# First batch fetched by whole slots, the first weight quarter between its loads, the others behind a gate

One core of one Trainium2 chip. The metric is the device time of one execution in microseconds (us); shorter is better.

## The reference

```python
X = np.fft.fft(x, axis=1)           # x: 8 batches of 3008 rows of 256
X = np.fft.fft(X, axis=2).real
h = np.maximum(X.reshape(24064, 256) @ w_in, 0.0)   # w_in: 256 x 2048
out = h * h @ w_out                                 # w_out: 2048 x 256
```

The kernel folds each batch by symmetry (a row is added to its mirror row), does the first transform as matmuls with cosine and sine tables ("first stage", tiles `pf`), puts the second transform into the weights (`G`, made from `w_in` by the `pc`/`ps` matmuls), multiplies by `G` (`xb`), squares, and multiplies by `w_out` (`po`).

## The kernel before

`x4` holds a batch in four slots: 0 and 1 are the upper rows of each half (fetched by SP), 2 and 3 the mirror rows (gathered by GpSimd). A fold adds slot `s` to slot `3 - s`, so slots 0 and 3 are the first pair and 1 and 2 the second.

```python
    for q in (0, QH):                          # two halves of three rows per partition
        for s in range(2):
            gather_half(0, 1 - s, QH - q)      # 378 KB, 3 KB rows
            nc.sync.dma_start(out=x4[0:NP, s, q : q + QH, :], in_=up(0, s, q, QH))
        if q == 0:
            load_mid(0, nc.sync)
            ...
    # fold_ops(0): for each half h, both pairs, then what hangs on that half
    return [[pair(0, h), pair(1, h), pair0(h * QH, QH), half(h, 0), edges(0, h * QH, QH)]
            + [feat(i, h * QH, QH) for i in (0, 2)] for h in range(2)], odd
    ...
    for f in mi0[0:0] + [dmats_fin, lambda: load_w_in(0, 1, 2, 3)] + mi0[0:] + [dmats_hi] + fe[0]:
        f()
    for f in rd1[0:0] + fe[1][0:3] + [lambda: load_x(1)] + fe[1][3:]:
        f()
    load_w_out()                               # GpSimd's queue, behind batch 1's gathers
    ...
    gcast(0, nc.scalar.copy)
    ...
    s1[0](); warm_up(2); gmat(0); s1[1](); s1[2]()    # first half, weight quarter 0, second half
```

The `po` matmuls of an output tile are ordered so:

```python
            cut = NFC if grp is final else NFC - 2 * nf
            ops += [one(grp, j, fc) for fcs in (range(cut), range(cut, NFC))
                    for j in range(len(grp)) for fc in fcs]
```

## Time and profile before

| | before |
|---|---|
| time, first chip | 606.13 us median of 4 (605.12 to 606.29) |
| profiled execution | 604.28 us, faster than all four of these; span 602.2 us, of which TensorE 581.0 busy |
| last gather of batch 0 landed | 16.48 us |
| first stage starts / first `xb` matmul | 13.40 / 21.51 us |
| `w_out` pieces landed | 36.89, 38.28, 39.64, 41.02 us |
| third group of four `po` matmuls | 39.98 us |

Landings are the completion records in the trace: each gather and each piece of `w_out` has 16 of them (here and there one is missing), and the last one counts.

### The profile page before, as it was taken

How to read it: one execution, taken by the hardware profiler on the slowest of the kernel's cores; microseconds unless marked ns; L12 is line 12 of the kernel's file. 1: busy time of each engine (PE TensorE's matmuls, PEld its weight loads, DVE VectorE, ACT ScalarE, POOL GpSimd, SP SyncE). 2: the span in 40 equal slices, each digit the busy share in tenths (PEclk: the TensorE clock that was granted, in tenths of full speed). 3: DMA queues.
4: the chain of work that ended last, by engine and by line, in shares of the span. 5: the costliest groups of instructions: out<-in, count | busy, mean ns of one | idle time of the engine just before them, and what ended most of it. 6: DMA issues, size and time to landing. Idle time of an engine off the chain costs nothing.

```text
span 602.2 us, 12242 instructions
## 1 busy us (share of the span) xinstructions
PE 581.0 (96%) x4543; PEld 436.9 (73%) x4543; DVE 522.6 (87%) x959; ACT 548.6 (91%) x963; POOL 164.4 (27%) x156
## 2 busy tenths in 40 slices
PE   2879999999999999999999999999999999999997
PEld 1556677777777777777777778777787778877786
DVE  6888898998898998898898997899889899999880
ACT  7789899999989999989998989999998999999981
POOL 5301022023322122312023043412443423324400
PEclk9989999999999999999999999999999999999999
DMA  8985484564483414913233115133242231332112
GB/s 237 283 105 155 109 238 149 175 234 54 63 246 54 62 46 73 244 41 45 56 60 45 53 38 63 42 45 58 58 63 41 50 53 54 44 62 56 56 53 71
DMA packets 42232, 56.24 MB, mean 93 GB/s; under 512 B 7774, under 2 KB 36754, under 8 KB 42174
## 3 DMA queue, kind: packets, MB, share of 16 engines
q1 hardware_dynamic: 37310, 42.04, 33.0%
q0 software_dynamic: 4864, 13.44, 8.7%
q8 instruction: 35, 0.57, 0.4%
q14 instruction: 23, 0.19, 0.1%
HBM read 29.02 MB, written 24.64 MB: 89 GB/s over the span
## 4 chain that ended last, share of the span: by engine, by line
PE 91%; DMA 4%; ACT 1%; POOL 1%; issue 1%; DVE 1%; POOLq 0%; ACTq 0%; DVEq 0%
PE po L74 54%; PE xb L74 31%; PE pf L74 6%; DMA wout<-in_moe_w_out_dram 3%; DMA x<-in_x_dram,idx 2%; POOL x L99 0%; POOL x L112 0%; ACT h L747 0%; ACT os L618 0%; ACT h L726 0%; ACT bs L713 0%; DVE bs L716 0%; DVE h L727 0%; DVE h L697 0%; ACT h L748 0%
## 5 line engine op out<-in xcount | busy, mean ns | idle before, releaser
L74 PE MATMUL po<-wout,h 128*128 128x256 f16 x3024 | 451.1, 273 | 3.5 <-DMA wout<-in_moe_w_out_dram 3.0
L74 PEld LDWEIGHTS <-h 128*128 128x128 f16 x3024 | 286.5, 98 | 113.8 <-issue 5.0
L74 PE MATMUL xb<-qt,G 128*128 128x512 f16 (+10 forms) x743 | 207.7, 322 | 1.3 <-ACT h L671 1.0
L714 POOL TENSOR_TENSOR bs<-bs,h 128x512 f32<-128x512 f32 x92 | 118.6, 1292 | 316.0 <-ACT bs L713 254.8
L727 DVE CUSTOM_DVE_ANT_0 h<-xb,bs 128x512 f16<-128x512 f32 (+1 forms) x231 | 144.6, 638 | 22.9 <-ACT h L726 22.1
L74 PE MATMUL xb<-pt,G 128*128 128x512 f16 (+16 forms) x512 | 146.7, 324 | 1.0 <-DVE h L727 0.4
L726 ACT ACTIVATE h<-xb 128x512 f16<-128x512 f32 (+1 forms) x218 | 135.4, 623 | 7.8 <-PE xb L74 5.5
L74 PEld LDWEIGHTS <-G 128*128 128x128 f16 x1255 | 120.5, 98 | 24.2 <-issue 2.8
L750 DVE TENSOR_TENSOR h<-h 128x2048 f16<-128x2048 f16 (+1 forms) x113 | 137.0, 1214 | 0.8 <-ACT h L738 0.7
L671 ACT ACTIVATE h<-xb 128x512 f16<-128x512 f32 (+1 forms) x166 | 103.8, 629 | 9.3 <-PE xb L74 8.4
L738 ACT ACTIVATE h<-xb 128x512 f16<-128x512 f32 (+2 forms) x155 | 95.8, 622 | 10.1 <-PE xb L74 8.5
L716 DVE SCALAR_TENSOR_TENSOR bs<-xb,h 128x512 f32<-128x512 f32 (+1 forms) x126 | 82.9, 659 | 18.7 <-PE xb L74 15.4
L748 ACT ACTIVATE h<-h 128x1024 f16<-128x1024 f16 (+1 forms) x79 | 84.8, 1074 | 0.0
L747 ACT ACTIVATE h<-h 128x1024 f16<-128x1024 f16 (+1 forms) x79 | 83.6, 1059 | 0.1
L697 DVE TENSOR_SCALAR h<-eb,gE 128x512 f16<-128x512 f16 (+1 forms) x198 | 69.9, 368 | 0.0
L618 ACT ACTIVATE os<-po 128x512 f32<-128x512 f32 (+1 forms) x95 | 59.5, 626 | 8.9 <-PE po L74 8.9
L713 ACT ACTIVATE bs<-xb 128x512 f32<-128x512 f32 x92 | 57.3, 623 | 3.2 <-PE xb L74 2.0
L112 POOL DMA_INDIRECT x<-in_x_dram,idx x16 | 21.0, 1314 | 78.8 <-DVE u L364 62.0
L360 DVE TENSOR_TENSOR u<-x 127x765 f16<-127x765 f32 x32 | 30.2, 965 | 3.5 <-DMA x<-in_x_dram,idx 3.5
L74 PEld LDWEIGHTS <-w 127*128 127x128 f16 (+1 forms) x192 | 22.1, 119 | 7.7 <-DVE w L373 2.2
L373 DVE TENSOR_TENSOR w<-v 127x384 f16<-127x384 f16 x64 | 22.1, 369 | 0.0
L74 PE MATMUL pf<-cosT,w 127*128 127x377 f16 (+1 forms) x96 | 20.6, 329 | 1.3 <-DVE w L373 1.3
(111 smaller groups left out, 212.5 us busy)
## 6 DMA issues: line engine op xcount, KB each, us to landing
out_dram<-os SPq DMA_DIRECT2D x157, 128.0 KB
x<-in_x_dram SPq DMA_DIRECT2D x14, 756.0 KB
wst<-in_moe_w_in_dram SPq DMA_DIRECT2D x4, 512.0 KB
eb<-qt SPq DMA_DIRECT2D x14, 128.0 KB
x<-in_x_dram SPq DMA_DIRECT2D x4, 378.0 KB
wout<-in_moe_w_out_dram POOLq DMA_DIRECT2D x4, 256.0 KB, 17.3
x<-in_x_dram,idx POOLq DMA_INDIRECT x20, 9.6
gE<-G SPq DMA_DIRECT2D x16, 0.2 KB
```

The source lines that it names most:

```text
L74: nc.tensor.matmul(o, l, r, start=start, stop=stop, skip_group_check=True)
L618: act(os_[:, js], po[:, js], AF.Copy, bias=0.0, scale=HS * HS)
L671: act(r_s(c, u), xb, AF.Relu, scale=-1.0)
L697: ts(out=X, in0=ebc[c][:, 0:n], scalar1=gE2[:, u : u + 1], scalar2=None, op0=ALU.mult)
L714: nc.gpsimd.tensor_tensor(T, T, X, op=ALU.add)
L716: stt(out=T, in0=xb, scalar=-2.0, in1=X, op0=ALU.mult, op1=ALU.add)
L726: act(r_s(c, u), xb, AF.Relu, scale=-1.0)
L727: mirrors.append((int(DEFER[c][u]), lambda: relu_d(c, u, lambda o, i: nc.vector._custom_dve(TENSOR_ADD_SAT, out=o[:, 0, :], in0=xb[:, 0, i ...
L738: relu_d(c, u, lambda o, i: act(o, xb[:, :, i], AF.Relu, scale=-1.0))
L747: act(h2[:, 0:nf], h2[:, 0:nf], AF.Square)
L748: rest.append(lambda: act(h2[:, nf:], h2[:, nf:], AF.Square))
L750: vt(h2, h2, h2, op=ALU.mult)
```

## The change

Its intent: longer rows for the first batch's loads, the weight that TensorE needs first brought in earlier, and the other weights kept from competing with the batch.

```diff
-    for q in (0, QH):
-        for s in range(2):
-            gather_half(0, 1 - s, QH - q)
-            nc.sync.dma_start(out=x4[0:NP, s, q : q + QH, :], in_=up(0, s, q, QH))
-        if q == 0:
+    for s in range(2):
+        gather(0, 1 - s)
+        nc.sync.dma_start(out=x4[0:NP, s, :, :], in_=up(0, s))
+        if s == 0:
             load_mid(0, nc.sync)
+            load_w_in(0)
 ...
-            return [[pair(0, h), pair(1, h), pair0(h * QH, QH), half(h, 0), edges(0, h * QH, QH)]
+            return [([pair(0, 0), pair(0, 1)] if h == 0 else [])
+                    + [pair(1, h), pair0(h * QH, QH), half(h, 0), edges(0, h * QH, QH)]
 ...
+    def w_gate():
+        for c in range(1, 4):
+            nc.vector.memset(wst[c][:, 0, 0:1], 0.0)   # the loads must wait for these writes
+        load_w_in(1, 2, 3)
 ...
-    for f in mi0[0:0] + [dmats_fin, lambda: load_w_in(0, 1, 2, 3)] + mi0[0:] + [dmats_hi] + fe[0]:
+    for f in mi0[0:0] + [dmats_fin] + mi0[0:] + [dmats_hi] + fe[0][:2] + [w_gate] + fe[0][2:]:
         f()
-    for f in rd1[0:0] + fe[1][0:3] + [lambda: load_x(1)] + fe[1][3:]:
+    for f in rd1[0:0] + fe[1][0:2] + [lambda: load_x(1)] + fe[1][2:]:
```

(Cut: the scratch tile moved from weight buffer 0 to 1, one index vector gone, a rewritten list that has the same values.)

More of the change, by code (lines that the diff above doesn't have):

```diff
@@ L80, in iota @@
         return t
-    idx3 = iota("idx3", [P, 1], [[0, 1]], NQ // QH * (NP - 1), -(NQ // QH), I32)
+    idx = iota("idx", [P, 1], [[0, 1]], NP - 1, -1, I32)
     pidx = iota("pidx", [P, 1], [[0, 1]], 0, 1)
@@ L96, in up @@
                        ap=[[NQ * D, NP], [1, n * D]])
-    def gather_half(b, s, q):
-        nc.gpsimd.indirect_dma_start(
-            out=x4[0:NP, 2 + s, q : q + QH, :].rearrange("p q d -> p (q d)"),
-            out_offset=None,
-            in_=bass.AP(tensor=x.tensor, offset=x.offset,
-                        ap=[[QH * D, B * S // QH], [1, QH * D]]),
-            in_offset=bass.IndirectOffsetOnAxis(ap=idx3[0:NP, 0:1], axis=0),
-            element_offset=(b * S + (s + 1) * M - NQ * NP + q) * D)
     def gather(b, s):
@@ L140, with load_w_in @@
     wst = [h2p.tile([P, 2, F // 4], F32, name="wst", tag="h2") for _ in range(4)]
-    jm = wst[0].rearrange("p c f -> p (c f)")[:, 0 : 3 * P].rearrange("p (a b) -> p a b", a=3)
-    for q in (0, QH):
-        for s in range(2):
-            gather_half(0, 1 - s, QH - q)
-            nc.sync.dma_start(out=x4[0:NP, s, q : q + QH, :], in_=up(0, s, q, QH))
-        if q == 0:
+    jm = wst[1].rearrange("p c f -> p (c f)")[:, 0 : 3 * P].rearrange("p (a b) -> p a b", a=3)
+    def load_w_in(*quarters):
+        for c in quarters:
+            cs = slice(c * F // 4, (c + 1) * F // 4)
+            nc.sync.dma_start(out=wst[c],
+                              in_=moe_w_in[:, cs].rearrange("(c p) f -> p c f", p=P))
+    for s in range(2):
+        gather(0, 1 - s)
+        nc.sync.dma_start(out=x4[0:NP, s, :, :], in_=up(0, s))
+        if s == 0:
             load_mid(0, nc.sync)
+            load_w_in(0)
             jrow = jm[:, 0]
@@ L150 @@
                            allow_small_or_imprecise_dtypes=True)
-    idx = iota("idx", [P, 1], [[0, 1]], NP - 1, -1, I32)
     idx2 = iota("idx2", [P, 1], [[0, 1]], NQ // 2 * (NP - 1), -NQ // 2, I32)
@@ L755 @@
     rd1, tr1, mi1 = table_ops(1)
-    def load_w_in(*quarters):
-        for c in quarters:
-            cs = slice(c * F // 4, (c + 1) * F // 4)
-            nc.sync.dma_start(out=wst[c],
-                                in_=moe_w_in[:, cs].rearrange("(c p) f -> p c f", p=P))
+    def w_gate():
+        for c in range(1, 4):
+            nc.vector.memset(wst[c][:, 0, 0:1], 0.0)
+        load_w_in(1, 2, 3)
     def load_w_out():
@@ L825 @@
     for c in range(1, F // 512):
-        side.setdefault(c * (c - 1) // 2, []).extend([lambda c=c: gmat(c), lambda c=c: gneg(c)])
+        side.setdefault((0, 1, 3)[c - 1], []).extend([lambda c=c: gmat(c), lambda c=c: gneg(c)])
     spread(rd1[0:], 0, 5)
```

## The prediction

> **What bounds the kernel now.** I read the page's busy shares first, then its chain of work that ended last, then that chain in order of time for the first 45 us, then the timelines of VectorE and TensorE there, and a table of windows over the same stretch.
>
> ```profile
> PE 581.0 (96%) x4543; PEld 436.9 (73%) x4543; DVE 522.6 (87%) x959; ACT 548.6 (91%) x963; POOL 164.4 (27%) x156
> ...
> PEclk9989999999999999999999999999999999999999
> DMA  8985484564483414913233115133242231332112
> ...
> PE 91%; DMA 4%; ACT 1%; POOL 1%; issue 1%; DVE 1%; POOLq 0%; ACTq 0%; DVEq 0%
> ```
>
> TensorE is busy for 581.0 of 602.2 us, so only 21 us are idle in all. The change touches only the load and fold of the first batch and the load of the first weight, so only the first 42 us can change, and at best they give back a part of those 21 us. A gain of 2% (12 us) is out of reach from here. The chain of work tells what rules this head:
>
> ```profile
> 5.29 9.62 DMA x<-in_x_dram,idx
> ...
> 17.85 1.22 POOL x L112
> 19.37 1.03 POOL x L112
> 20.40 0.83 POOL wout L766
> 21.23 17.05 DMA wout<-in_moe_w_out_dram
> 38.28 0.04 issue
> 38.33 1.01 PE po L74 x4
> ```
>
> From 5 us to 38 us it is transfers: the first batch, then its slots are free and batch 1 is fetched, then w_out queues up behind batch 1's gathers. TensorE waits for w_out here:
>
> ```profile
> 34.27 0.27 PE L74 MATMUL xb<-qt,G 128*128 128x256 f16 x1
> 36.93 0.60 PE L74 MATMUL po<-wout,h 128*128 128x256 f16 x4 [2.39 <-DMA wout<-in_moe_w_out_dram]
> ...
> 38.33 1.01 PE L74 MATMUL po<-wout,h 128*128 128x256 f16 x4 [0.58 <-DMA wout<-in_moe_w_out_dram]
> ...
> 41.27 0.77 PE L74 MATMUL po<-wout,h 128*128 128x256 f16 x4
> ```
>
> The four pieces of w_out landed at 36.89, 38.28, 39.64 and 41.02 us (landing records of the trace), and the groups of four po matmuls start at 36.93, 38.33, 39.98 and 41.27. So the fourth piece pins TensorE to about 41.3 us, whatever happened before. The windows say that the transfer engines were full all the way, and that the wait let the clock drop:
>
> ```profile
> core 0: us, PE busy (x) PEld busy (x) DVE busy (x) ACT busy (x) POOL busy (x), PEclk, DMA share, GB/s
> ...
> 21.50:34.50 13.00, 11.58 (x84) 8.18 (x84) 12.86 (x24) 12.70 (x24) 2.13 (x3) 1.00 1.20 228
> 34.50:38.30 3.80, 0.86 (x7) 0.58 (x6) 3.77 (x11) 3.80 (x9) 0.00 (x0) 0.99 1.29 157
> 38.30:41.60 3.30, 3.27 (x16) 2.28 (x16) 2.50 (x9) 2.61 (x8) 0.00 (x0) 0.50 0.46 39
> ```
>
> [...] while both queues have work (6 to 14 us) they share some 260 GB/s, and a 3 KB packet of the SP queue takes 121 ns alone (median, 2 to 4 us) and 167 ns beside gathers (9 to 13 us). [...] Here the granted clock goes to full at 17.7 us, and is 0.50 in 38.2 to 41.6, after the w_out wait. [...] the 127x765 fold takes 955 ns whatever the row length of its load, so the change makes no fold cheaper. [...] the 128x128 int32 operation took 1.70 us at 7.93, ending as the zeroing of ez (7.90, 1.39 us) was over.
>
> **The change, part by part.** On VectorE only the order changes, as the two kernels' instruction orders show; the only additions are three 128x1 memsets (60 ns each, as the one at 1.40 us), 0.2 us in the shade of a DMA wait. TensorE and ScalarE keep their order; the rearranged list of weight groups (0, 1, 3) equals c(c-1)/2.
>
> Loads. Before, SP issues four 378 KB pieces, GpSimd four gathers; now two of 756 KB each. GpSimd saves two gathers of 1.0 to 1.1 us. The bytes are the same (3.1 MB). Packets of gathers were already 6 KB for the most part; SP's grow from 3 KB to 6 KB. In batch 2's load at 52 us, SP's 6 KB rows alone ran at 234 ns a packet (26 GB/s per engine) against 25 GB/s for 3 KB rows, and 289 GB/s over whole microseconds, against 353. So I count no gain from longer rows. What counts is the order of bytes. First pair: up to 5.4 us SP's slot (before, the two half slots landed at 4.34 and 5.46), with the gather complete at some 8.2 to 9 us (774 KB from 4.3 us, at some 200 GB/s beside the smaller weight packets). Second pair: it must follow 3.1 MB and 0.52 MB of the first weight quarter. Before, the transfers had moved 3.62 MB at 14.2 us and the last gather landed at 16.48. I put the second pair at 14.7 us (estimate, 14.2 to 15.5): about 1.8 us earlier, as three weight quarters (issued at 10.16 before) no longer share.
>
> Folds. Before, the last piece cost one pair fold: 16.50 + 0.95 + 0.18 + 0.56 + 0.17 + 0.62, with overlaps, 18.88.
>
> ```profile
> 14.94 0.95 DVE L360 TENSOR_TENSOR u<-x 127x765 f16<-127x765 f32 x1 [1.33 <-DMA x<-in_x_dram,idx]
> 16.50 0.95 DVE L360 TENSOR_TENSOR u<-x 127x765 f16<-127x765 f32 x1 [0.60 <-DMA x<-in_x_dram,idx]
> 17.37 0.18 DVE L364 TENSOR_TENSOR u<-x 127x6 f16<-127x6 f32 x1
> 17.58 0.56 DVE L369 TENSOR_TENSOR v<-u 127x768 f16<-127x768 f16 x1
> ```
>
> Now both halves' folds follow the last landing: 2 x (0.95 + 0.18 + 0.56 + 0.17 + 0.62) = 5.0 us, less small overlaps. First half ready (its first feature) at 14.7 + 2.2 = 16.9, second at 19.6. So TensorE's first stage starts at 16.9 instead of 13.40, cold: nine matmuls of 0.31 us, two warm-ups of 0.43, four weight matmuls of 0.43, nine more: 8.2 us at half clock, some 6.4 us [...]. It ends at 23.3 us instead of 21.3: a loss of 2.0 us there. The first weight quarter, for which ScalarE sat idle 3.8 us, lands early; that wait goes.
>
> Slots. Batch 1's load is issued when the last pair fold and its edge are done: 14.7 + 0.1 + 3.6 = 18.4 against 17.58. But before, three quarters of a megabyte of weights were still queued in front of it; now some 0.1 MB is. Bytes up to then: 5.19 MB (batch and weights) moved at 19.7 us before, and now at 18.5, with up to 1 us of hole until batch 1's first packet (an SP load took 1.0 us from issue to packet, a gather 2.3). From there w_out ends a chain of the same bytes. If bytes decide, w_out's last piece comes about 0.5 us sooner; if the gathers' late start decides, 0.8 us later. I take 0.5 sooner, 40.5 us.
>
> Sum. TensorE reaches its first w_out wait at 34.5 + 2.0 = 36.5, so the 2 us lost in the first stage are taken out of a wait of 3.0 us and cost nothing; the idle stretch gets shorter, and the clock probably stays full. TensorE after the fourth piece: 41.27 before (with 0.16 us more lost until the clock rose at 41.6), 40.6 now: some 0.9 us gained. 606.16 - 0.9 = 605.2 us.
>
> **Rivals.** (a) TensorE becomes the bound: first piece used at 36.5 or later, then 2.2 us of work at full clock to the fourth group, 38.7. Only if w_out comes over 1.8 us sooner does this matter; it caps the gain at 2.7 us: 603.5. For it: 0.65 MB less backlog before batch 1, at 300 GB/s 2 us. Against it: the hole, and batch 1's gathers, that needed until 35.87 to land. (b) The late slots win: gathers of batch 1 start with the slots at 18.4 to 19.5 and w_out keeps its 23.5 us distance (17.55 to 41.02): 41.9, a loss of 0.5: 606.7. For it: gathers crept at 6 to 61 KB per us for the first four us even when their queue had work. (c) The second pair lands no earlier than 16.5, since 6 KB rows of both queues beside each other ran at 240 to 250 GB/s in 22 to 28 us with 390 ns a packet: then everything is 1.8 us later, TensorE reaches po at 38.3, and w_out too comes later: up to 607.5.
>
> **Range and chances.** The mechanisms move the fourth piece by +1 to -2 us; (b) and (c) bound one side, (a) the other[...]. Range 603.6 to 606.9. Faster by over 2% needs 12 us, more than the head's idle time holds: 1%. Slower by 2%: 1%. Within 2%: 98%.
>
> **What would show it.** Right: the pair folds at some 9 and 10 us and again at 15; first stage start near 17; no ScalarE wait for the weight; batch 1 issued near 18.4; the TensorE wait for w_out down from 3.0 to under 1.5 us with no half clock near 40; fourth w_out piece at 40 to 41. Wrong: the second pair after 16.5, w_out's fourth piece later than 41.5, or a new wait of TensorE between 23 and 36 us (a weight quarter not there, as they were gated).

## More of the kernel before

All that matters here happens in the first 45 us. From there on TensorE is nearly always busy: from the third group of `po` matmuls to the end, the fourteen traces of this study take 561.5 to 562.9 us.

## The result

The changed kernel took 606.8 us (median of 4, 606.3 to 607.13) against 606.13. The ratio of fast runs is 1.0014, with a 95% interval of 0.9997 to 1.0031: the same at 2%, and not a gain. On another chip, with 6 and 11 runs, it was 607.31 against 604.33, ratio 1.0055 (1.0039 to 1.0071): slower by 3.3 us. A ratio here is the mean time of one kernel's fast runs over that of the other's of the same rounds, so not quite the ratio of the medians. I take the second as the better measure, with more runs. On the chips of the three sets below the kernel before had medians of 604.04, 604.33 and 603.05, and its profiled execution took 604.28, so its four runs at 606.1 were probably on its slow side and flatter the change; as chips may differ, that is likely and not shown.

The page of the changed kernel: busy shares, slices, and the chain by engine.

```profile
PE 579.3 (96%) x4543; PEld 436.1 (72%) x4543; DVE 524.1 (87%) x962; ACT 547.7 (91%) x963; POOL 163.1 (27%) x153
...
DMA  8793685674484314913133115133342231332112
...
PE 87%; DMA 5%; ACT 4%; DVE 1%; POOL 1%; issue 1%; ACTq 0%; DVEq 0%; POOLq 0%
```

TensorE has less busy time (579.3 against 581.0, as less of it ran slowly: at a clock of 0.50 from 20.8 to 23.8 us, where before its matmuls were as slow from 13.4 to 17 us and the clock was 0.50 from 38.2 to 41.6) in a longer span (604.5 against 602.2). ScalarE's part of the chain grew from 1% to 4%. One of the waits of the first 46 us (engine, line, what it waited for, us in total, times, longest):

```profile
PE po L74 <- DMA wout<-in_moe_w_out_dram: 0.9, 3, 0.4
```

The wait for `w_out` fell from 3.0 to 0.9 us, as forecast. But TensorE sat idle 11.1 us for the first fold. VectorE's folds and TensorE's first stage in order of time (start, duration; in brackets the idle time before it, and what ended that):

```profile
10.06 1.81 DVE L356 TENSOR_TENSOR u<-x 127x765 f16<-127x765 f32 x2
11.82 0.08 DVE L756 MEMSET wst<- 128x1 f32 x3
18.60 0.96 DVE L356 TENSOR_TENSOR u<-x 127x765 f16<-127x765 f32 x1 [6.70 <-DMA x<-in_x_dram,idx]
...
20.97 0.95 DVE L356 TENSOR_TENSOR u<-x 127x765 f16<-127x765 f32 x1
```

```profile
20.84 1.13 PE L74 MATMUL pf<-cosT,w 127*128 127x377 f16 x3 [11.12 <-DVE w L369]
...
26.87 0.27 PE L74 MATMUL xb<-pt,G 128*128 128x256 f16 x1 [0.26 <-DVE pt L490]
...
42.80 0.60 PE L74 MATMUL po<-wout,h 128*128 128x256 f16 x4 [0.36 <-DMA wout<-in_moe_w_out_dram]
```

The same three points of TensorE in the kernel before:

```profile
13.40 1.12 PE L74 MATMUL pf<-cosT,w 127*128 127x377 f16 x3 [1.31 <-DVE w L373]
...
21.51 0.27 PE L74 MATMUL xb<-pt,G 128*128 128x256 f16 x1 [0.26 <-DVE pt L493]
...
39.98 1.06 PE L74 MATMUL po<-wout,h 128*128 128x256 f16 x4
```

The second pair landed at 18.58 us, 2.1 us later than the last gather before. The first stage starts 7.4 us later and the first `xb` 5.4 us later. The third `po` group is at 42.80 instead of 39.98, and that difference of 2.8 us, less some 0.8 that the kernel before lost there at half clock (an estimate: half of the 1.6 us from 39.98 until its clock rose at 41.6), is most of the 2.3 us between the two spans. The windows of the two kernels, before first and the changed one after it (window, length, busy time of TensorE, its weight loads, VectorE, ScalarE and GpSimd, clock, share of the transfer engines, GB/s). In the first line the clock of 1.00 is no reading up to 17.7 us, since the trace's clock records start there:

```profile
16.00:19.50 3.50, 1.99 (x8) 0.70 (x7) 2.93 (x7) 1.14 (x2) 1.34 (x2) 1.00 1.04 377
19.50:23.00 3.50, 2.98 (x18) 1.70 (x17) 2.14 (x6) 3.20 (x6) 3.50 (x5) 1.00 1.00 267
```

```profile
16.00:19.50 3.50, 0.00 (x0) 0.00 (x0) 0.90 (x2) 0.00 (x0) 0.00 (x0) 0.50 0.99 321
19.50:23.00 3.50, 2.16 (x7) 1.19 (x8) 3.29 (x12) 0.00 (x0) 0.68 (x1) 0.50 0.23 85
```

Before, the transfers were full all the way (share 1.04 and 1.00). Now there is a hole at 19.5 to 23 us (share 0.23): the weights are all but through (0.15 MB of packets after 20 us) and batch 1 is not asked for before 22.0 us, since the late folds still hold its slots. Everything behind the hole, `w_out` last, comes about 3 us later (third piece 42.76 instead of 39.64).

### The profile page after: what moved, and what is told of

It is laid out like the page before. It is cut to its first block, busy times and chain, and to the rows that moved or that the text cites. A ratio compares the mean times of both kernels' runs of the same rounds, so it can differ in the third digit from the quotient of the medians.

```text
span 604.5 us, 12238 instructions
## 1 busy us (share of the span) xinstructions
PE 579.3 (96%) x4543; PEld 436.1 (72%) x4543; DVE 524.1 (87%) x962; ACT 547.7 (91%) x963; POOL 163.1 (27%) x153
## 4 chain that ended last, share of the span: by engine, by line
PE 87%; DMA 5%; ACT 4%; DVE 1%; POOL 1%; issue 1%; ACTq 0%; DVEq 0%; POOLq 0%
PE po L74 52%; PE xb L74 30%; PE pf L74 6%; DMA wout<-in_moe_w_out_dram 3%; DMA x<-in_x_dram,idx 2%; ACT h L723 1%; ACT h L744 1%; POOL x L103 1%; ACT h L745 1%; ACT os L615 0%; ACT bs L710 0%; DVE h L724 0%; DVE u L356 0%; POOL wout L762 0%; DVE h L694 0%
## 5 line engine op out<-in xcount | busy, mean ns | idle before, releaser
L103 POOL DMA_INDIRECT x<-in_x_dram,idx x18 | 24.0, 1332 | 83.2 <-DVE u L360 66.0
L74 PE MATMUL pf<-cosT,w 127*128 127x377 f16 (+1 forms) x96 | 20.7, 329 | 11.1 <-DVE w L369 11.1
```

The costliest lines, as they stand in the source:

```text
L74: nc.tensor.matmul(o, l, r, start=start, stop=stop, skip_group_check=True)
```

## The experiments

Two explanations of the loss had to be told apart: `w_out` lands late because of the hole (transfers), or TensorE's first stage is late and nothing hides it any more (compute). And for the late second pair: weights let in too early, long rows, or the order of slots. Twelve kernels ran, all correct, five rounds each, in three sets of four, each set on one chip. Ratios are to the kernel before on that chip. The set's chip had it at a median of 604.04 (first), 604.33 (second) and 603.05 (third).

**1. The gate one fold later**, in the changed kernel: no quarter but the first can move before the second pair is in.

```diff
-    ... + fe[0][:2] + [w_gate] + fe[0][2:]:
+    ... + fe[0][:3] + [w_gate] + fe[0][3:]:
```

> The changed kernel with its gate moved one fold later, behind the first fold of the second pair, so that no other weight quarter can start before that pair is in. Theory A (weights let in too early): the changed kernel's last gather landed at 18.6 us because the gate opened at 11.8 us and 0.97 MB of weights moved ahead of it; without them 3.62 MB at 273 KB per us land at about 15 us, first stage of TensorE near 17.5 us (20.84 in the changed kernel), the hole in the transfers at 20 to 23 us gone, third piece of w_out near 40 us instead of 42.8, time 1 to 2 us under the changed kernel. Rival B (6 KB rows are slow): last gather stays at 17.5 us or later and the time within 0.5 us of the changed kernel.

Ratio 1.0078 (1.0055 to 1.0100), 609.24 us: the slowest of all. The second pair landed at 16.66 instead of 18.58, so early weights did cost 1.9 us. But that is far from 15 us, and the time went the other way. Its windows:

```profile
12.00:16.00 4.00, 0.00 (x0) 0.00 (x0) 0.00 (x0) 3.53 (x9) 0.00 (x0) 1.00 0.67 212
16.00:19.50 3.50, 0.55 (x2) 0.28 (x3) 2.68 (x10) 0.00 (x0) 0.00 (x0) 1.00 0.13 36
```

The hole did not vanish; it moved forward and grew, because the weights were asked for only after the landing (the gate opened at 17.59 us) and their traffic began at 18.8 us and filled the transfer engines only from 19.5 us. The first stage was 1.9 us earlier than in the changed kernel (18.95), the third `po` group later (43.9, behind a `w_out` wait of 2.3 us and at half speed: `xb` matmuls 0.21 us apart after it, 0.11 before). An earlier first stage is worth nothing while `w_out` comes late.

**2. The first weight quarter behind both slots**, in the changed kernel.

```diff
         if s == 0:
             load_mid(0, nc.sync)
-            load_w_in(0)
             ...
+    load_w_in(0)
```

> The changed kernel with the first weight quarter issued behind both slots instead of between them; gate as it is. Theory A counts bytes: half a megabyte less ahead of the second pair, so it lands at about 16.6 us instead of 18.6; time about 1 us under the changed kernel, the hole shorter by 1 to 2 us. Rival B (row length): no change of the landing beyond 0.5 us.

Ratio 1.0043 (1.0023 to 1.0062). The second pair landed at 16.19, 2.4 us sooner and so the expected size, the hole shrank to about 1.2 us, first `xb` 24.95, third `po` group 40.3. Its profiled execution (604.85 us) was its fastest; its other five were at 606.4 to 607.8. It is within 0.12% of the control in the next set, on another chip, so no gain in time over the changed kernel is shown.

**3. Half slots in 3 KB rows**, in the changed kernel: four loads and four gathers, in the same order of slots.

```diff
-        gather(0, 1 - s)
-        nc.sync.dma_start(out=x4[0:NP, s, :, :], in_=up(0, s))
+        for q in (0, QH):
+            gather_half(0, 1 - s, QH - q)
+            nc.sync.dma_start(out=x4[0:NP, s, q : q + QH, :], in_=up(0, s, q, QH))
```

> The changed kernel with each slot loaded as two halves in 3 KB rows, in the same order of slots, weight and gate as it is. Theory A: rows do not matter, last gather at 18 to 19.5 us, time within 0.7 us of the changed kernel. Rival B: last gather at 16.5 us or earlier, and about 1 us faster than the changed kernel.

Ratio 1.0013 (0.9994 to 1.0032), on the chip where edit 2 had 1.0043 and edit 1 had 1.0078. Both expectations missed. The last piece landed at 17.66, 0.9 us sooner. But the fold did not wait for it:

```profile
15.63 0.95 DVE L367 TENSOR_TENSOR u<-x 127x765 f16<-127x765 f32 x1 [2.69 <-DMA x<-in_x_dram,idx]
...
18.00 0.95 DVE L367 TENSOR_TENSOR u<-x 127x765 f16<-127x765 f32 x1
```

A fold needs one half of each slot. When each half is its own transfer it starts when that half is in, at 15.63; with whole slots it waits for all of both, 18.60. So the first stage starts at 17.87 instead of 20.84. Whole slots cost 3.0 us here: some 2 by their grain, and 0.9 by the later landing. Whether that 0.9 is the row length or the gate, which opened at 12.87 us here and at 11.82 in the changed kernel, was not separated. Long rows alone do not make the landing late: edit 2 has them and landed at 16.19.

**4. The gate alone**, in the kernel before: quarters 1 to 3 behind the last pair fold.

```diff
-    ... [dmats_fin, lambda: load_w_in(0, 1, 2, 3)] ...
+    ... [dmats_fin, lambda: load_w_in(0)] ...
-    ... fe[1][0:3] + [lambda: load_x(1)] ...
+    ... fe[1][0:2] + [w_gate] + fe[1][2:3] + [lambda: load_x(1)] ...
```

> The kernel before with only the gate added: weight quarters 1 to 3 wait for the last pair fold. Theory A: last gather at about 14.7 us instead of 16.5, second half of the fold done near 17 us; but the transfers were full before and stay full, so w_out comes no earlier (third piece at 39.6, within 0.7 us) and the time stays within 0.6 us of the kernel before. Rival C (the end is set by how late the folds and the first stage are): 1.5 to 2 us faster than the kernel before.

Ratio 1.0044 (1.0023 to 1.0064). The last gather landed at 16.55 instead of 16.48: keeping the weights out gained nothing at all. A gather counts as landed with its last share: its 16 completions came in from 13.30 to 16.55 us. A hole of some 3 us opened between 15.5 and 19 us, and TensorE waited 3.65 us for the fourth quarter, which now landed at 29.9. Both expectations missed: the landing did not move, and the time got worse by 2.9 us. (The same loads landed at 16.48, 16.65 and 15.73 us in three executions, so differences under 1 us in one trace are noise; the changed kernel had 18.58, 18.47 and 18.49.)

**5 and 6. `w_out` ahead of batch 1**, in the kernel before and in the changed kernel.

```diff
+    def w_out_first():
+        for c in range(4):
+            nc.vector.memset(wout16[:, c * NFC // 4, 0:1], 0.0)
+        load_w_out()
-    ... + [lambda: load_x(1)] + ...
+    ... + [w_out_first, lambda: load_x(1)] + ...
-    load_w_out()
```

A control, the changed kernel itself, ran beside them:

> The changed kernel once more, as a control on the same chip as the next runs. Ratio to the kernel before between 1.0005 and 1.003, as in the first result; third group of po matmuls at 42 to 43.5 us; a hole in the transfers at 20 to 23 us.

It had 1.0055, more than expected; its third `po` group was at 42.5 and the hole was there.

> The kernel before with w_out fetched ahead of batch 1's gathers (gated by one-column zeroings behind the last pair fold). Theory D (the end of the head is the third piece of w_out; what comes before it hides behind that wait): w_out lands before 33 us, TensorE waits for it no more, third group of po matmuls near 36 to 38 us instead of 40.0, 2 to 4 us faster than the kernel before (ScalarE and VectorE are full between 27 and 40 us, which eats a part of the 4.7 us). Rival C (the first stage sets the end already): no change beyond 0.7 us.

Ratio 0.9948 (0.9932 to 0.9964), 600.98 us, the best time. No `po` matmul waits for `w_out` any more, and the third group comes at 38.32.

> The changed kernel with the same edit. Theory D: the w_out wait (0.9 us) goes, but now the late first stage shows: xb matmuls from 26.9 us instead of 21.5, third group of po at about 41.4 us; 1 to 1.5 us faster than the changed kernel, and 3 to 5 us slower than the kernel before with the same edit. Rival (the late folds cost nothing even then): within 1 us of the kernel before with the same edit.

Ratio 1.0046 (1.0033 to 1.0058), 606.97 us: 0.1% under the control, and 6.0 us above the other. The chain of the changed kernel with this edit says what holds it:

```profile
29.30 0.49 ACT G L327
29.79 0.49 ACT G L328
...
42.44 0.56 ACT sinT L283
```

From the first `xb` on, nearly all of the chain is ScalarE's operations, one every 0.49 us. First `xb` to third `po` group took 15.0 us here, and 15.4 in the kernel before with the edit; the changed kernel's two lines first:

```profile
27.60 0.27 PE L74 MATMUL xb<-pt,G 128*128 128x256 f16 x1 [0.21 <-DVE pt L490]
...
42.60 0.60 PE L74 MATMUL po<-wout,h 128*128 128x256 f16 x4
```

```profile
22.90 0.31 PE L74 MATMUL xb<-pt,G 128*128 128x256 f16 x1
...
38.32 0.60 PE L74 MATMUL po<-wout,h 128*128 128x256 f16 x4
```

In the kernel before without the edit it took 18.5, since the wait for `w_out` is in it. This settles the main question. The kernel before was held by `w_out`. In the changed kernel the late first stage and the late `w_out` come out at nearly the same time (26.87 + 15.4 = 42.3, and 42.76), so removing one of them gains next to nothing. With `w_out` out of the way of both, all the 4.7 us between their first `xb` show: the two spans are 4.4 us apart (605.3 and 600.9), the timed medians 6.0.

**7. The same in the kernel before, but ungated**: `w_out` right behind the first batch's gathers.

```diff
-    ... fe[1][0:3] + [lambda: load_x(1)] + fe[1][3:]
+    ... [load_w_out] + fe[1][0:3] + [lambda: load_x(1)] + fe[1][3:]
```

> The kernel before with w_out issued at once behind the first batch's gathers, with no gate. Theory A (bytes let in too early delay the last landing): some of w_out moves before the last gather has landed, which comes 0.5 to 2 us later than 16.5 us, and the folds with it; w_out no longer waits behind batch 1, so still 1 to 3.5 us faster than the kernel before, but not faster than the gated form.

Ratio 0.9951 (0.9934 to 0.9968), not to be told from the gated form. The last gather landed at 16.90 (16.65 in the gated form), and the first `xb` came at 23.41 (22.90): both have the expected sign, but single traces of the same loads differ by as much, so no delay is shown.

**8 to 10. Which part makes the first stage late.** With `w_out` ahead of batch 1 the time follows the first `xb`, so the parts of the change were tried on that form. It ran again as the yardstick.

> The kernel before with w_out ahead of batch 1, once more as the yardstick on this chip: ratio to the kernel before near 0.995, first xb matmul near 22.9 us, third po group near 38.3 us.

Ratio 0.9966 (0.9939 to 0.9993), first `xb` at 21.91, third group at 37.34.

> The kernel before with one part of the change alone: the first weight quarter issued between the two halves of the first batch's loads, the other quarters as before, no gate. Theory D: ScalarE and TensorE no longer wait for this weight (3.8 and 1.5 us), the last gather lands 0.5 to 1 us later than 16.5 us, but w_out still comes behind the same bytes at about 39.7 us (third piece), so the time stays within 0.7 us of the kernel before. Rival C (the wait for the first weight is on the path): 1 to 1.5 us faster.

```diff
         if q == 0:
             load_mid(0, nc.sync)
+            load_w_in(0)
```

(and `load_w_in(1, 2, 3)` at the old place). This is the kernel before, with `w_out` where it was. Ratio 1.0034 (1.0011 to 1.0056): 2 us slower, neither of the two expectations. The profiled execution was its fastest by far (602.69; the others 604.4 to 606.5), so its trace doesn't explain the mean, and I leave that cause open. It does show the last packets of batch 0's SP loads at 16.6 us instead of 13.4, behind the weight.

> The same with w_out ahead of batch 1. With the w_out wait gone the first xb matmul sets the third po group 15.2 us later (measured: 22.90 to 38.3, 27.60 to 42.6, 26.97 to 42.5), so an earlier first xb shows in full: first xb at 21.0 to 22.3 us instead of 22.9, 0.5 to 1.5 us faster than the yardstick, if the last gather does not lose as much.

Ratio 1.0012 (0.9991 to 1.0034), 0.46% above the yardstick (the intervals just touch); the opposite of what I expected. The last fold shows why:

```profile
18.88 0.95 DVE L367 TENSOR_TENSOR u<-x 127x765 f16<-127x765 f32 x1 [1.92 <-DMA x<-in_x_dram]
```

It starts at 18.88 instead of 15.76, and the releaser is now SP's own load, queued behind the weight. The first `xb` came at 23.86 instead of 21.91. The weight was early, the batch late, and the batch is what TensorE needs.

> The yardstick with the order of slots and folds of the changed kernel alone: 3 KB rows, weights behind the loads and ungated as before, w_out ahead of batch 1. Theory D: both halves are folded behind the last loads, TensorE starts its first stage at 16.5 to 18 us instead of 13.4, first xb at 23.5 to 25 us, and the time is 1 to 2 us above the yardstick (the changed kernel with w_out ahead was 5.9 us above it: the rest is gate, weight between and long rows). Rival (the order of slots is harmless): within 0.5 us of the yardstick.

The edit: half slots in the order of slots, folds in the changed order, weights ungated and behind the loads as before. Ratio 0.9995 (0.9973 to 1.0016), 603.23 us: 0.29% or 1.1 to 1.8 us above the yardstick, as expected, though the two intervals overlap. First stage at 16.45 instead of 14.06, first `xb` at 23.50 instead of 21.91:

```profile
16.45 1.13 PE L74 MATMUL pf<-cosT,w 127*128 127x377 f16 x3 [4.37 <-DVE w L379]
```

The order alone makes the first half wait for a later gather. The remaining way to 20.74 us, where the changed kernel with `w_out` ahead starts its first stage, is gate, weight and whole slots together.

## Why the prediction was wrong

It named the size of the stake rightly (nothing near 2%) and had the sign wrong: 0.9 us of gain forecast, 0.7 us (not clear of noise) and 3.3 us (clear) of loss measured. By its own steps:

- **"I put the second pair at 14.7 us": failed, and carries the rest.** It landed at 18.58. The step read off when 3.62 MB had moved in a kernel whose transfers were kept full by later loads. It misread even that: 233 GB/s over the first 14.2 us make 3.3 MB, and 238 GB/s over the first 15.2 us make 3.62, so the mark was 15.2 and not 14.2 us, which alone would move the estimate to about 15.7. It also held that the queued weights would no longer share. They did: the gate opens after the first pair, at 11.8 us, long before the second is in. That was worth 1.9 us (edit 1). The half megabyte between the loads was worth 2.4 us (edit 2); the two overlap and do not add up. And with the three quarters kept out the last gather still landed at 16.6 us (edits 1 and 4), as a transfer's shares finish at different times: the 16 completions of the changed kernel's last gather came in over 5.2 us (13.38 to 18.58), and over 4.0 us in edit 1 (12.71 to 16.66). Why they end so far apart was not tested.
- **First stage 2.2 us after the landing, then 6.4 us: right.** Measured 2.2 (18.60 to 20.84) and 6.0 (20.84 to 26.87), half of it at half clock (0.50 until 23.8 us). The 6.4 was the author's estimate. It is only the start that was 4 us off. So "a loss of 2.0 us there" was 5.4 us.
- **"The 2 us lost in the first stage are taken out of a wait of 3.0 us and cost nothing": the mechanism was right, the size not.** The wait did shrink, to 0.9 us. But 5.4 us do not fit in 3.0. The way between, which the prediction moved one for one, did so: first `xb` to the first wait for `w_out` is 13.0 us before (21.51 to 34.54) and 13.0 in the changed kernel (26.87 to 39.91). ScalarE fills it (busy 12.70 of the 13.0 us from 21.5 before, 12.50 of the 12.8 from 26.9 in the changed kernel), and first `xb` to third group is 15.0 to 15.4 us in all six kernels that wait neither for `w_out` nor for a weight on the way.
- **"Up to 1 us of hole", batch 1 asked for at 18.4: mis-sized.** Asked for at 22.0 to 22.3; a hole of about 3 us. So `w_out` came 3.1 us later and not 0.5 sooner.
- **"The fourth piece pins TensorE": wrong.** The code above shows that three pieces serve two row tiles before the fourth is used. The third piece is the last that can hold TensorE here. In the changed kernel it did (landed 42.76, used 42.80); before, it had landed 0.34 us before its use (39.64 and 39.98), with TensorE at half clock (0.50 from 38.2 us) after the waits for the first two pieces (2.39 and 0.58 us).
- **The clock stays full near 40 us, no ScalarE wait for the weight: right.** The half clock near 40 us is gone (1.00 in 39.7 to 43 us, 0.71 before). The first nine matmuls of the first stage run slowly in both kernels, about 0.31 us apart against 0.16 later in the stage (from 13.40 us before, from 20.84 in the changed kernel, where the clock record says 0.50; the clock is full from 17.7 and from 23.8 us).
- **Rival (c)** described the outcome: second pair at 16.5 or later, everything later, up to 607.5. It gave the slowness of long rows as its cause. What the third edit shows is rather their grain: one completion for what two folds need at different times.

## What to carry to other kernels

Ask for each load which instruction needs how much of it, and give that much its own completion; a longer row was worth nothing here, as the first consumer then waited for the last byte (the fold of the second pair at 18.60 us against 15.63). A gate that keeps later loads out can open a hole behind itself if the transfers run dry before it lets them in: both gates on the weights that opened after the landing did so here (no transfer from 16.5 to 18.5 us in edit 1, from 17 to 18.5 in edit 4), and these two have the highest ratios of their set (1.0078 and 1.0044). And before moving a load forward, find the load at the end of the queue that the critical engine really waits for: moving `w_out` ahead of batch 1 gained 0.3 to 0.5%, more than any edit of the first batch.

## What else the traces show

- Full transfer engines did not mean an early start: with 756 KB in place of 378 KB per load the first stage started 3.0 us later here (20.84 against 17.87), while the engines' share was 0.99 in 16 to 19.5 us. The completions of one 756 KB gather lay 2.9 us (edit 2) to 5.2 us (changed kernel) apart in these runs.
- A 6 KB packet of the SP queue took 234 ns alone (median, 52 to 54 us in the kernel before), and 390 ns beside the gathers' queue (22 to 28 us).
- Two VectorE operations ran long beside GpSimd's work. One fp32 tensor_scalar took 2.43 us in the changed kernel (from 5.05 us) where it took 0.45 before, while GpSimd went from a gather's issue (until 5.43 us) straight through its zeroings (until 7.18 us). The 128x128 int32 operation took 1.70 us in the kernel before (7.93 to 9.63 us), where GpSimd zeroed `ez` from 7.90 to 9.29 us, and 0.22 in the changed kernel (9.87). What held them was not tested. The first cost little: the first folds began at 10.06 us, 0.6 us after their gather (9.47), and the next fold waited 6.7 us for the second pair anyway.
